# Attention and two gated MLPs on one core: v of the first batch loaded in contiguous pieces, transfer rates in the planner's prices, weight sums on VectorE, own tiles for the last results

## Chip, cores and metric

One NeuronCore of a Trainium2 chip runs the whole program in one launch. The metric is the device time of one execution in microseconds; lower is better. Engines are TensorE (PE), VectorE (DVE), ScalarE (ACT), GpSimd (POOL) and SyncE (SP, which issues most transfers).

## The reference

Three stages in float32 over 8 batches of 576 tokens. First linear attention with 8 heads of 64:

```python
q_s = softmax(q, axis=head_dim)
k_s = softmax(k, axis=seq)
kv = einsum('bhsd,bhse->bhde', k_s, v)
x = einsum('bhsd,bhde->bhse', q_s, kv)      # heads joined: x is [8, 576, 512]
```

Then an MLP with a gate that mixes the tokens:

```python
h = gelu(x @ w_in)                          # [576, 1024], halves u and v
v_n = (v - mean) / sqrt(var + 1e-6) * g_ln
v_s = einsum('ts,bsd->btd', w_sg, v_n) + b_sg
x = x + (u * v_s) @ w_out
```

Then one with a convolution of 3 taps along the tokens as its gate:

```python
h = relu(x @ w_in2)                         # [576, 1024]
out = (h * sigmoid(conv3(h, conv_w))) @ w_out2
```

## The kernel before

Every product keeps float32 accuracy by splitting each operand into a high and a low part and adding three products (`mm3`, line 472). So weights and activations must be split before PE can use them: ACT rounds the high part, another engine subtracts it to get the low part (names end in h and l).

Phase 1, up to about 562 us, runs attention and the first MLP batch by batch. Phase 2 runs the second MLP. There, batches 0 and 1 multiply by w_in2 directly (`h2`, line 1229). Batches 2 to 7 use a scheme of seven instead of eight block products (`quad`, line 1420); it needs sums of blocks of the weights, which `weight_sums(c)` (line 1327, for c = 0 and 1) forms once while batches 0 and 1 are still being computed: 4 sums high + low (`tk<-w2h,w2l`), 4 differences (`tk<-tk,tk`), then 3 splits into tn0, tn1, tn2, of which ACT makes the high and POOL the low part. That makes 11 operations on POOL for each c.

No engine's order is written by hand. The program calls engines through recorders; a planner (class `Plan`, lines 149 to 424) keeps every operation as a node with its dependences, prices it (`price`, line 216), derives due times backwards from the end (`deadlines`), and simulates all engines and the transfer lanes to choose at each moment what each engine takes next (`order`, line 280). `emit` (line 417) then issues the real instructions in that order. So nearly all instructions show the line of `emit`, L424, and are told apart by tile names here; and a change of one price can move instructions on every engine. A load on SP is priced at 1.9 us + KB / 200 (line 225), and the lanes are taken as busy for KB / 200 (line 339).

At the start, k of batch 0 is loaded in four tiles (sgl), q in five (sgh), v in one (vt, `load_v(0)`, line 897), then the weights (vnh, vnl, xh, xl, wsl are buffers that weights are staged in). The tile vt has 65 columns for each head, the last one holds ones, so that v fills 64 of 65 columns: its load writes into strided places. DVE takes maxima and sums for the softmaxes (sm), POOL subtracts and multiplies on q (sgh), PE transposes q (acc<-one,sgh; `s_qt`, line 949). Then `back_kv` (line 702) multiplies k and v (mm<-vt,kt), `xt` (line 743) multiplies by q, and `w_job` (line 1009) splits the weights of the first MLP in pieces, with PE, ACT, DVE and POOL taking part (on PE: mm<-vnh,one with mm<-wAh,neg). The first product of that MLP is mm<-wAh,xh.

At the end, `evac` (line 1261) copies each finished block of the result from PSUM to a tile ot, of which there are two, by turns on ACT and DVE, and SP stores it. The last block comes out in five such pieces.

Of the kernel before, what the change touches and what calls it, by code (L numbers as in the profile page):

```python
# [11 lines left out]
F32 = mybir.dt.float32  # L12
# [13 lines left out]
CFG = {'dord': 'qqkqqkqwkkwwv', 'start': 'kaaatabbktbkbqkTawtqbqtQvwwvxxqxswxlwLc', 'gh': 'aaa', 'x2': 'nnn', 'hvl': [6, 5, 3], 'qs': 'ppppd', 'qm': 'pppdp', 'vb': 2, 'gb': 2, 'kt': 'dddd', 'sgl': 'dppp', 'rh': 'pd', 'sw': 'ada', 'sl': 'ada', 'gl': 'ddd'}  # L26
FAR = 90.0
FIRST = 2
SUMS = ((0, 6), (1, 2))
YB = 4  # L30
GUARD = 1.125 * 2.0 ** -15
# [103 lines left out]


class Node:
    __slots__ = ("eng", "name", "args", "kw", "cost", "lat", "deps", "succ", "late", "unit", "shared", "table", "kb", "i", "left", "ready", "done", "t", "hook", "due")


class Engine:
# [7 lines left out]
class Plan:  # L149
# [66 lines left out]
    def price(self, n, out, ins):  # L216
        size = lambda v: int(np.prod(v.shape[1:]))
        views = ins + ([out] if isinstance(out, View) else [])
        cols = max(size(v) for v in views)
        psum = any(v.tile.space == "psum" for v in views)  # L220
        e, name = n.eng, n.name
        if e == "sp":
            v = views[0]
            n.kb = v.ids.size * 4 / 1024
            n.cost, n.lat = 0.42, 1.9 + n.kb / 200
        elif e == "pe":
            m = size(out)
            if name == "transpose":
                n.cost = 0.22
            elif ins[0].tile.dtype == F32:  # L230
                n.cost = 0.09 if m == 65 else 0.71 if m == 512 else 0.19
            else:
                n.cost = max(0.111, 0.0045 + m * 0.000447)
            n.lat = n.cost + 0.17
        elif e == "act":
            n.cost = (0.155 if psum else 0.195) + cols * 0.00085
            if isinstance(n.kw.get("scale"), View) or isinstance(n.kw.get("bias"), View):
                n.cost += 0.05 + min(cols, 500) * 0.0001
            n.lat = n.cost + 0.07
            f = args_func(n)  # L240
            n.table = {"Gelu_apprx_tanh": "g", "Exp": "e", "Sigmoid": "s"}.get(f)
        elif e == "pool":
            if "dma" in name:
                n.cost, n.lat = 1.2, 20.0
                return
            if "tensor" in name:
                wide = any(o[0] == "to_broadcast" for v in views for o in v.ops)
                n.cost = 0.95 if cols == 1 else 0.2 + cols * (0.0008 if name == "tensor_copy" else 0.00164 if wide else 0.0021)
            else:
                n.cost = 0.05 + cols * 0.0009  # L250
            n.lat = n.cost + 0.1
            n.shared = True
        else:
            two = sum(v.tile.space != "psum" for v in ins) > 1 and not psum and name in ("tensor_tensor", "scalar_tensor_tensor")
            fast = not psum and name in ("tensor_scalar", "tensor_copy") and out.tile.dtype == F32
            n.cost = 0.15 + cols * (0.0062 if name == "reciprocal" else 0.00055 if fast else 0.00104)
            if len(ins) > 2 or (fast and len(ins) > 1):
                n.cost += min(cols, 500) * 0.00013
            n.lat = n.cost + 0.07
            n.shared = (two or fast) and cols > 60  # L260
# [19 lines left out]
    def order(self):  # L280
# [41 lines left out]
        def start(n, t):  # L322
            cost, lat = n.cost, n.lat
            if n.eng == "act" and n.table and n.table != table[0]:
                cost, lat, table[0] = cost + 1.28, lat + 1.28, n.table
            if n.eng == "dve" and n.shared and poolend[0] > t:
                more = min(cost, poolend[0] - t) * 1.0
                cost, lat = cost + more, lat + more
            if n.eng == "pool":
                if vecend[0] > t:  # L330
                    more = min(0.5, vecend[0] - t)
                    cost, lat = cost + more, lat + more
                poolend[0] = t + cost
            if n.eng == "dve" and n.shared:
                vecend[0] = t + cost
            if n.eng == "sp":
                heapq.heappush(events, max(t, wire[0] - 1.0) + 0.01)
                s = max(t + 0.4, wire[0])
                wire[0] = s + n.kb / 200
                lat = wire[0] + 1.9 - t  # L340
                heapq.heappush(events, wire[0] - 0.99)
            n.t, n.done = t, t + lat
            free[n.eng] = t + cost
            out.append(n)
            heapq.heappush(events, free[n.eng])
            heapq.heappush(events, n.done)
            release(n, "start", t)
            release(n, "end", n.done)
# [84 lines left out]
def attn_gated_conv_kernel(ctx, tc, q, k, v, q0, k0, w_in, g_ln, w_sgT, b_sg, w_out, w_in2, conv_w, w_out2, out):  # L433
# [144 lines left out]
    def load_q(b):  # L578
        for c in range(4):
            sp.dma_start(q_tile(b, c), q[b, :, c * 512:c * 512 + 512])  # L580
# [4 lines left out]
    def load_v(b):  # L585
        sp.dma_start(vt[:, :, :, 0:64], v[b])
# [307 lines left out]
        sp.dma_start(k0t[:, hps[i]], k0[:, hps[i]])  # L894
    for i in range(5):
        sp.dma_start(q0t[:, qts[i]], q0[:, qts[i]])
    load_v(0)

    for e in range(2):
        pool.memset(r32(rhs2[e]), 0.0)  # L900
# [96 lines left out]
    for hp in range(4):  # L997
        s_qt(hp)
    s_qtl()
    load_q(1)  # L1000
    load_left(1)
    s_xl()
# [4 lines left out]
    xt_left(0)  # L1007
    xt_copy(0)
    def w_job(i):
        split(slots[ORDER[i]], *jobs[i], None)  # L1010

    ORDER = (4, 5, 0, 1, 2, 3, 0, 1, 2, 3, 0, 1)
    for i in range(4):
# [5 lines left out]

    def sg_split(c):  # L1020
        act.activation(sg["hi"][:, c], sgs[:, c % 2], AF.Copy)
        for hf in range(2):
            cs = slice(hf * HALF, hf * HALF + HALF)
            plan.begin()
            ps = mm_tile()[:, 0:HALF]
            part(ps, sgs[:, c % 2, cs], sg["hi"][:, c, cs])
            act.activation(sg["lo"][:, c, cs], ps, AF.Copy)
        if c < 3:
            sg_load(c + 2)
# [216 lines left out]
    def gate(b, fc, h, cv):  # L1246
# [11 lines left out]
        dve.tensor_tensor(zl, cv[:, 512:S], r32(zh), ALU.subtract)  # L1258
        y_t[b, fc] = (yh, yl)

    def evac(ps, dst, i=0):
        ot = p2.tile([128, DM], F32, tag="ot", bufs=2)
        if i % 2:
            dve.tensor_copy(ot, ps)
        else:
            act.activation(ot, ps, AF.Copy)
        for rows, d in dst:
            sp.dma_start(d, ot[rows])
# [58 lines left out]
    def weight_sums(c):  # L1327
        after = plan.last
        w11, w12, w21, w22, w3 = (tmp() for _ in range(5))
        for t, n in zip((w11, w12, w21, w22), ("11", "12", "21", "22")):  # L1330
            pool.tensor_tensor(t, r32(wq[n][0][:, c]), r32(wq[n][1][:, c]), ALU.add).deps[after.i] = "start"
        pool.tensor_tensor(w11, w12, w11, ALU.subtract)
        pool.tensor_tensor(w3, w22, w12, ALU.subtract)
        pool.tensor_tensor(w22, w22, w11, ALU.subtract)
        pool.tensor_tensor(w21, w21, w22, ALU.subtract)
        for t, (hi, lo) in zip((w11, w22, w21), tn):
            act.activation(hi[:, c], t, AF.Copy)
            pool.tensor_tensor(lo[:, c], t, r32(hi[:, c]), ALU.subtract)
        last.append(w3)

    def last_sum():
# [144 lines left out]
    while len(oq) > 1:  # L1486
        do_o()
    o2_pair(B - 1, range(NFC - 1))
    do_o()
    o2_pair(B - 1, [NFC - 1])  # L1490
    plan.emit()
# [52 lines left out]
```

## Time and profile before

| what | value |
|---|---|
| median of 3 runs | 963.08 us (961.0 to 966.03) |
| the profiled execution | 961.07 us |
| its span in the profile | 959.2 us (1.87 us lie outside) |
| PE busy | 926.0 us (97%), 6026 matmuls |
| DVE busy | 775.2 us (81%), 1455 instructions |
| ACT busy | 540.8 us (56%), 1113 instructions |
| POOL busy | 347.6 us (36%), 351 instructions |
| granted TensorE clock | 0.998 |
| transfers | 99.16 MB, lanes 35% busy |

Each execution ends when the slowest engine has ended and the last store has landed. Because PE is busy for 97% of the span, the time is PE's work plus PE's idle time; a stage in which another engine is nearly full shows where PE may have to wait. A row of a timeline tells the start in us, the duration, engine, line, operation, output<-input by tile names, and in brackets the idle time of that engine just before it and who ended it.

### The profile page before, as it was taken

How to read it: one execution, taken by the hardware profiler on the slowest of the kernel's cores; microseconds unless marked ns; L12 is line 12 of the kernel's file. 1: busy time of each engine (PE TensorE's matmuls, PEld its weight loads, DVE VectorE, ACT ScalarE, POOL GpSimd, SP SyncE). 2: the span in 40 equal slices, each digit the busy share in tenths (PEclk: the TensorE clock that was granted, in tenths of full speed). 3: DMA queues.
4: the chain of work that ended last, by engine and by line, in shares of the span. 5: the costliest groups of instructions: out<-in, count | busy, mean ns of one | idle time of the engine just before them, and what ended most of it. 6: DMA issues, size and time to landing. Idle time of an engine off the chain costs nothing.

```text
span 959.2 us, 16062 instructions
## 1 busy us (share of the span) xinstructions
PE 926.0 (97%) x6026; PEld 818.8 (85%) x6026; DVE 775.2 (81%) x1455; ACT 540.8 (56%) x1113; POOL 347.6 (36%) x351
## 2 busy tenths in 40 slices
PE   5999989999999999999999999999999999999996
PEld 4568877989988889888899998888989889988985
DVE  6987899889879889898766359998788968896773
ACT  6775553745646456737533225445666756766662
POOL 5425354555626636646543030851211202020000
PEclk9999999999999999999999999999999999999999
DMA  9551524182473553813457671002111211021001
GB/s 280 163 185 56 163 71 112 51 208 52 154 178 102 162 138 114 212 39 118 92 162 207 198 213 51 35 12 71 35 50 44 73 33 68 26 72 34 23 23 55
DMA packets 54246, 99.16 MB, mean 103 GB/s; under 512 B 5268, under 2 KB 28820, under 8 KB 52376
## 3 DMA queue, kind: packets, MB, share of 16 engines
q1 hardware_dynamic: 50472, 89.88, 30.0%
q0 software_dynamic: 3696, 8.26, 4.8%
q8 instruction: 47, 0.77, 0.3%
q14 instruction: 31, 0.25, 0.1%
HBM read 62.59 MB, written 35.53 MB: 102 GB/s over the span
## 4 chain that ended last, share of the span: by engine, by line
PE 74%; DVE 15%; ACT 4%; DMA 3%; issue 2%; SPq 0%; POOL 0%; ACTq 0%; DVEq 0%
PE mm L424 50%; PE acc L424 24%; DVE cv L424 4%; DMA wsl<-in_w_in 2%; DVE wsl L424 2%; DVE xl L424 1%; DVE scr L424 1%; DVE yl L424 1%; ACT L424 1%; DVE gl L424 1%; DVE vnl L424 1%; DVE sm L424 1%; DMA sgh<-in_q 0%; ACT vnh L424 0%; DVE lx L424 0%
## 5 line engine op out<-in xcount | busy, mean ns | idle before, releaser
L424 DVE SCALAR_TENSOR_TENSOR cv<-h,cw,cv 128x576 f32<-128x576 f32 x128 | 120.0, 937 | 22.1 <-ACT cv L424 20.5
L424 PE MATMUL acc<-wAh,yl 128*128 128x512 f32 x256 | 101.9, 398 | 1.2 <-DVE yl L424 1.2
L424 PE MATMUL acc<-wAh,yh 128*128 128x512 f32 x256 | 101.1, 395 | 1.5 <-ACT yh L424 1.2
L424 PE MATMUL acc<-wAl,yh 128*128 128x512 f32 x256 | 101.1, 395 | 0.0
L424 PE MATMUL mm<-xh,w2h 128*128 128x288 f32 x280 | 82.9, 296 | 0.0
L424 PE MATMUL mm<-xl,w2h 128*128 128x288 f32 x280 | 82.4, 294 | 0.0
L424 PE MATMUL mm<-xh,w2l 128*128 128x288 f32 x280 | 82.4, 294 | 0.0
L424 PE MATMUL mm<-sgh,vnh 128*128 128x288 f32 x256 | 81.2, 317 | 1.1 <-DVE u L424 0.8
L424 PE MATMUL mm<-xh,wAh 128*128 128x288 f32 x256 | 79.7, 311 | 2.0 <-DVE xl L424 1.2
L424 PE MATMUL acc<-gh,wouth 128*128 128x288 f32 x256 | 80.9, 316 | 0.0
L424 ACT ACTIVATE cv<-cv 128x576 f32<-128x576 f32 x64 | 43.7, 683 | 62.7 <-DVE cv L424 62.6
L424 PE MATMUL acc<-gl,wouth 128*128 128x288 f32 x256 | 76.3, 298 | 0.7 <-DVE gl L424 0.6
L424 PE MATMUL mm<-sgh,vnl 128*128 128x288 f32 x256 | 75.7, 296 | 0.8 <-DVE vnl L424 0.8
L424 PE MATMUL acc<-gh,woutl 128*128 128x288 f32 x256 | 75.8, 296 | 0.0
L424 PE MATMUL mm<-xh,wAl 128*128 128x288 f32 x256 | 75.5, 295 | 0.0
L424 PE MATMUL mm<-xl,wAh 128*128 128x288 f32 x256 | 75.5, 295 | 0.0
L424 PE MATMUL mm<-sgl,vnh 128*128 128x288 f32 x256 | 75.4, 294 | 0.0
L424 POOL TENSOR_TENSOR q<-q,qm 128x512 f32<-128x512 f32 x56 | 61.6, 1125 | 26.1 <-DVE qm L424 22.2
L424 POOL TENSOR_TENSOR wsl<-wsl 128x256 f32<-128x256 f32 (+1 forms) x66 | 48.4, 733 | 57.9 <-DVE wsl L424 31.9
L424 POOL TENSOR_TENSOR kt<-kt,scr 128x512 f32<-128x512 f32 (+1 forms) x42 | 48.5, 1181 | 49.5 <-PE mm L424 24.0
L424 ACT ACTIVATE gh<-u 128x288 fp32r<-128x288 f32 x64 | 28.2, 441 | 67.3 <-DVE u L424 67.1
L424 POOL TENSOR_TENSOR xf<-xf 128x576 f32<-128x576 f32 x12 | 21.8, 1821 | 118.9 <-DVE xl L424 90.2
(276 smaller groups left out, 2960.3 us busy)
## 6 DMA issues: line engine op xcount, KB each, us to landing
vt<-in_v SPq DMA_DIRECT2D x8, 1152.0 KB, 8.9
x2d<-x2s SPq DMA_DIRECT2D x16, 576.0 KB, 3.8
out<-ot SPq DMA_DIRECT2D x32, 256.0 KB, 2.1
kt<-in_k SPq DMA_DIRECT2D x7, 1152.0 KB, 5.3
x2d<-xl POOLq DMA_DIRECT2D x7, 1152.0 KB, 11.2
xf<-x2d SPq DMA_DIRECT2D x7, 1152.0 KB, 5.9
q<-in_q SPq DMA_DIRECT2D x28, 256.0 KB, 3.0
wsl<-in_w_in SPq DMA_DIRECT2D x16, 256.0 KB, 3.7
```

The source lines that it names most:

```text
L424: getattr(self.real[n.eng], n.name)(*[val(a) for a in n.args], **{k: val(v) for k, v in n.kw.items()})
```

## The change

The planner gives each transfer a rate of its own: 125 KB per us for the strided load of v into vt, 250 for all others, in place of 200 for all. The v of batch 0 is loaded in five contiguous pieces into buffers that later hold q (tags q0 to q4), and `v_stage` copies them into vt with five copies on POOL. The sums of the weights are made on DVE (`WS`) instead of POOL. For the last result's five pieces, `evac` takes own tiles, which are slices of the operand buffers xf and xg, instead of ot. `JOBS` and `SGL` hold only 'n' and leave `w_job` and `sg_split` as they were (their hunks are left out here).

```diff
@@ -26,6 +26,10 @@
...
 FAR = 90.0
 FIRST = 2
+WS = 'd'
+JOBS = 'nnnnnnnnnnnn'
+SGL = 'nnnn'
+VST = 'pppp'
 SUMS = ((0, 6), (1, 2))
 YB = 4
 GUARD = 1.125 * 2.0 ** -15
@@ -222,7 +226,8 @@
         if e == "sp":
             v = views[0]
             n.kb = v.ids.size * 4 / 1024
-            n.cost, n.lat = 0.42, 1.9 + n.kb / 200
+            n.rate = 125 if any(o[0] == '__getitem__' and len(o[1]) > 3 for o in v.ops if isinstance(o[1], tuple)) and v.tile.key.startswith('vt') else 250
+            n.cost, n.lat = 0.42, 1.9 + n.kb / n.rate
         elif e == "pe":
             m = size(out)
             if name == "transpose":
@@ -336,7 +341,7 @@
             if n.eng == "sp":
                 heapq.heappush(events, max(t, wire[0] - 1.0) + 0.01)
                 s = max(t + 0.4, wire[0])
-                wire[0] = s + n.kb / 200
+                wire[0] = s + n.kb / n.rate
                 lat = wire[0] + 1.9 - t
                 heapq.heappush(events, wire[0] - 0.99)
             n.t, n.done = t, t + lat
@@ -894,7 +899,20 @@
         sp.dma_start(k0t[:, hps[i]], k0[:, hps[i]])
     for i in range(5):
         sp.dma_start(q0t[:, qts[i]], q0[:, qts[i]])
-    load_v(0)
+    vst = [(4 * c, at.tile([128, 512 if c < 4 else 256], F32, tag=f"q{c}", bufs=2)) for c in range(5)]
+    for c, (g, t) in enumerate(vst):
+        n = min(4, 18 - g)
+        sp.dma_start(t, v[0, :, g:g + n].rearrange("p g e d -> p (g e d)"))
+
+    def v_stage():
+        for c, (g, t) in enumerate(vst):
+            n = min(4, 18 - g)
+            dst_, src_ = vt[:, g:g + n, :, 0:64], t.rearrange("p (g e d) -> p g e d", g=n, e=2)
+            if VST[min(c, 3)] == 'a':
+                act.activation(dst_, src_, AF.Copy)
+            else:
+                E[VST[min(c, 3)]].tensor_copy(dst_, src_)
+
     for e in range(2):
         pool.memset(r32(rhs2[e]), 0.0)
@@ -997,6 +1015,7 @@
     for hp in range(4):
         s_qt(hp)
     s_qtl()
+    v_stage()
     load_q(1)
     load_left(1)
     s_xl()
@@ -1258,8 +1279,13 @@
         dve.tensor_tensor(zl, cv[:, 512:S], r32(zh), ALU.subtract)
         y_t[b, fc] = (yh, yl)
+    out_t = []
+
     def evac(ps, dst, i=0):
-        ot = p2.tile([128, DM], F32, tag="ot", bufs=2)
+        if out_t:
+            ot = out_t.pop()
+        else:
+            ot = p2.tile([128, DM], F32, tag="ot", bufs=2)
         if i % 2:
             dve.tensor_copy(ot, ps)
         else:
@@ -1328,14 +1354,14 @@
         after = plan.last
         w11, w12, w21, w22, w3 = (tmp() for _ in range(5))
         for t, n in zip((w11, w12, w21, w22), ("11", "12", "21", "22")):
-            pool.tensor_tensor(t, r32(wq[n][0][:, c]), r32(wq[n][1][:, c]), ALU.add).deps[after.i] = "start"
-        pool.tensor_tensor(w11, w12, w11, ALU.subtract)
-        pool.tensor_tensor(w3, w22, w12, ALU.subtract)
-        pool.tensor_tensor(w22, w22, w11, ALU.subtract)
-        pool.tensor_tensor(w21, w21, w22, ALU.subtract)
+            E[WS].tensor_tensor(t, r32(wq[n][0][:, c]), r32(wq[n][1][:, c]), ALU.add).deps[after.i] = "start"
+        E[WS].tensor_tensor(w11, w12, w11, ALU.subtract)
+        E[WS].tensor_tensor(w3, w22, w12, ALU.subtract)
+        E[WS].tensor_tensor(w22, w22, w11, ALU.subtract)
+        E[WS].tensor_tensor(w21, w21, w22, ALU.subtract)
         for t, (hi, lo) in zip((w11, w22, w21), tn):
             act.activation(hi[:, c], t, AF.Copy)
-            pool.tensor_tensor(lo[:, c], t, r32(hi[:, c]), ALU.subtract)
+            E[WS].tensor_tensor(lo[:, c], t, r32(hi[:, c]), ALU.subtract)
         last.append(w3)
     def last_sum():
@@ -1486,6 +1512,8 @@
     while len(oq) > 1:
         do_o()
     o2_pair(B - 1, range(NFC - 1))
+    out_t.extend(p2.tile([128, KC, S], F32, tag="xf")[:, i, 0:512] for i in range(4))
+    out_t.append(p2.tile([128, S], F32, tag="xg")[:, 0:512])
     do_o()
     o2_pair(B - 1, [NFC - 1])
     plan.emit()
```

On SP, at the start of the program (sgl is k, sgh is q, vt and the tiles q are v, vnh and the rest are weights). Before:

```order
L424 DMA sgl_89<-in_k 128x576 x2
L424 DMA sgh_98<-in_q 128x512
L424 DMA vt_85<-in_v 128x36x64
L424 DMA sgh_98<-in_q 128x256
L424 DMA vnh_121<-in_w_in 128x1024
L424 DMA vnl_124<-in_w_in 128x1024
```

Now:

```order
L429 DMA sgl_89<-in_k 128x576 x2
L429 DMA sgh_98<-in_q 128x512
L429 DMA sgh_98<-in_q 128x256
L429 DMA q_0_119<-in_v 128x512
L429 DMA q_0_122<-in_v 128x512
L429 DMA q_0_126<-in_v 128x512
L429 DMA q_0_128<-in_v 128x512
L429 DMA q_0_130<-in_v 128x256
L429 DMA vnh_133<-in_w_in 128x1024
L429 DMA vnl_136<-in_w_in 128x1024
```

The fifth tile of q (128x256) stands ahead of v, and five issues of v stand where one stood, still ahead of the weights.

On DVE, at the start (sm<-sgh are maxima and sums of q; of the two in one row before, the first is the sum of the third tile, the second the maximum of the fourth, and in the new order these two have changed places). Before:

```order
L424 TENSOR_SCALAR sm_117<-sm_117 128x8
L424 TENSOR_REDUCE sm_117<-sgl_89 128x1
L424 TENSOR_REDUCE sm_117<-sgh_98 128x8
L424 TENSOR_REDUCE sm_117<-sgl_89 128x1
L424 TENSOR_REDUCE sm_117<-sgh_98 128x8 x2
L424 RECIPROCAL sm_117<-sm_117 128x8
```

Now:

```order
L429 TENSOR_REDUCE sm_117<-sgl_89 128x1
L429 TENSOR_REDUCE sm_117<-sgh_98 128x8
L429 TENSOR_REDUCE sm_117<-sgl_89 128x1
L429 TENSOR_REDUCE sm_117<-sgh_98 128x8 x2
L429 TENSOR_SCALAR sm_117<-sm_117 128x8
L429 RECIPROCAL sm_117<-sm_117 128x8
```

The small TENSOR_SCALAR has moved behind the maximum of q's fourth tile.

On DVE, in batch 1 of phase 2 (cv is the convolution, yh and yl the gated result, tk and tn the sums of the weights). Now:

```order
L429 TENSOR_TENSOR cv_5694<-cv_5694,h_0_4981 128x576
L429 TENSOR_TENSOR tk_5992<-w2h_4967,w2l_5005 128x512
L429 TENSOR_TENSOR tk_6000<-w2h_4967,w2l_5005 128x512
L429 TENSOR_TENSOR yl_5840<-cv_5694,yh_5823 128x512
L429 TENSOR_SCALAR cv_5742<-h_0_5662,cw_861 128x576
L429 SCALAR_TENSOR_TENSOR cv_5742<-h_0_5662,cw_861,cv_5742 128x576 x2
L429 TENSOR_TENSOR yLl_5777<-cv_5694,yLh_5752 128x64
L429 TENSOR_TENSOR tk_5992<-tk_6000,tk_5992 128x512
L429 TENSOR_TENSOR tk_6056<-w2h_4967,w2l_5005 128x512
```

These are the first sums: they stand in ones and twos between the steps of the convolution, from there on to the first block products of batch 2; before, no sum stood on DVE.

## Rows read from the trace of the kernel before

**Rows 1.** Windows: stretch; length, busy us (instructions) of each engine; clock, DMA share, GB/s
```profile
0.00:959.20 959.20, 926.04 (x6026) 818.84 (x6026) 775.21 (x1455) 540.80 (x1113) 347.61 (x351) 1.00 0.35 103
0.00:40.00 40.00, 27.50 (x156) 16.34 (x157) 31.24 (x61) 28.37 (x54) 18.02 (x30) 1.00 0.73 232
600.00:640.00 40.00, 38.74 (x227) 34.12 (x226) 39.55 (x35) 17.25 (x38) 31.84 (x20) 1.00 0.07 27
640.00:660.00 20.00, 20.00 (x117) 17.82 (x116) 19.31 (x29) 11.14 (x24) 3.75 (x2) 1.00 0.00 1
```

**Rows 2.** Timeline of ACT at the end: start, us, operation, [idle before <-releaser]
```profile
951.99 0.60 ACT L424 ACTIVATE ot<-acc 128x512 f32<-128x512 f32 x1 [2.15 <-DMA out<-ot]
954.73 0.60 ACT L424 ACTIVATE ot<-mm 128x512 f32<-128x512 f32 x1 [2.14 <-DMA out<-ot]
```

**Rows 3.** What PE waits for, 40 to 560 us: total us, times, longest
```profile
PE mm L424 <- DVE u L424: 2.8, 2, 2.0
```

**Rows 4.** Timeline of PE at the end
```profile
951.61 0.39 PE L424 MATMUL mm<-wAh,yLl 128*128 128x512 f32 x1
```

**Rows 5.** Groups on tile tk: min/median/max ns, first and last start
```profile
L424 POOL TENSOR_TENSOR tk<-w2h,w2l x8: 1300/1804/1816, 567.4 to 635.3; 128x512 f32<-128x512 f32 x8
```

**Rows 6.** Timeline of DVE, 566 to 576 us
```profile
566.22 4.89 DVE L424 SCALAR_TENSOR_TENSOR cv<-h,cw,cv 128x576 f32<-128x576 f32 x2
...
574.39 0.82 DVE L424 SCALAR_TENSOR_TENSOR cv<-h,cw,cv 128x576 f32<-128x576 f32 x1
575.12 0.68 DVE L424 TENSOR_TENSOR yl<-cv,yh 128x512 fp32r<-128x512 f32 x1
```

**Rows 7.** What PE waits for, 560 to 660 us
```profile
PE acc L424 <- DVE yl L424: 1.2, 2, 0.7
```

**Rows 8.** Timeline of PE near 576 us
```profile
575.86 0.50 PE L424 MATMUL acc<-wAh,yl 128*128 128x512 f32 x1 [0.70 <-DVE yl L424]
```

**Rows 9.** Timeline of SP at the start
```profile
4.50 0.68 SPq L424 DMA_DIRECT2D vt<-in_v  x1
5.23 7.49 SPq L424 DMA_DIRECT2D sgh<-in_q  x1
```

**Rows 10.** DMA issues of the first 22 us: count, KB, median us to landing
```profile
vt<-in_v SPq DMA_DIRECT2D x1, 1152.0 KB, 10.5
```

**Rows 11.** Windows at the start, columns as in rows 1
```profile
4.00:10.00 6.00, 2.09 (x8) 1.43 (x8) 5.05 (x9) 4.78 (x9) 4.59 (x6) 1.00 1.02 331
10.00:13.00 3.00, 2.04 (x9) 1.64 (x10) 2.97 (x9) 2.41 (x5) 0.47 (x1) 1.00 1.04 218
```

**Rows 12.** Timeline of DVE at the start
```profile
11.19 1.26 DVE L424 TENSOR_REDUCE sm<-sgh 128x8 f32<-128x512 f32 x2
...
15.88 1.25 DVE L424 TENSOR_TENSOR sgh<-sgh,sm 128x512 f32<-128x512 f32 x1
```

**Rows 13.** Timeline of POOL at the start
```profile
1.32 0.53 POOL L424 MEMSET kvd<- 128x512 f32 x1
...
12.53 4.04 POOL L424 TENSOR_TENSOR sgh<-sgh,sm 128x512 f32<-128x512 f32 x4 [3.20 <-DVE sm L424]
```

**Rows 14.** What PE waits for, 0 to 40 us
```profile
PE acc L424 <- POOL sgh L424: 2.1, 3, 1.0
PE mm L424 <- POOL xh L424: 0.8, 2, 0.6
PE mm L424 <- DVE xl L424: 0.5, 1, 0.5
```

**Rows 15.** Timeline of PE at the start
```profile
20.10 1.83 PE L424 MATMUL mm<-vt,kt 128*64 128x65 f32 x40
...
28.35 1.08 PE L424 MATMUL mm<-vnh,one 128*128 128x512 f32 x2
...
30.41 1.02 PE L424 MATMUL mm<-vnl,one 128*128 128x512 f32 x2
...
38.69 0.82 PE L424 MATMUL mm<-wAh,xh 128*128 128x512 f32 x1
```

More of the change, by code (lines that the diff above doesn't have):

```diff
@@ L137 @@
 class Node:
-    __slots__ = ("eng", "name", "args", "kw", "cost", "lat", "deps", "succ", "late", "unit", "shared", "table", "kb", "i", "left", "ready", "done", "t", "hook", "due")
+    __slots__ = ("eng", "name", "args", "kw", "cost", "lat", "deps", "succ", "late", "unit", "shared", "table", "kb", "i", "left", "ready", "done", "t", "hook", "due", "rate")
 class Engine:
@@ L1009, in w_job @@
     def w_job(i):
-        split(slots[ORDER[i]], *jobs[i], None)
+        split(slots[ORDER[i]], *jobs[i], None if JOBS[i] == 'n' else (E[JOBS[i]], E[JOBS[i]]))
     ORDER = (4, 5, 0, 1, 2, 3, 0, 1, 2, 3, 0, 1)
@@ L1021, in sg_split @@
         act.activation(sg["hi"][:, c], sgs[:, c % 2], AF.Copy)
-        for hf in range(2):
+        if SGL[c] != 'n':
+            E[SGL[c]].tensor_tensor(sg["lo"][:, c], sgs[:, c % 2], r32(sg["hi"][:, c]), ALU.subtract)
+        for hf in range(2 if SGL[c] == 'n' else 0):
             cs = slice(hf * HALF, hf * HALF + HALF)
```

## The prediction, on record before the changed kernel ran

> **What bounds the kernel now.** I read the busy times by stage first, then what TensorE (PE) waits for in each stage, then the single rows around those waits. PE is busy for 926.0 of 959.2 us, at a granted clock of 1.00 in every stage shown [rows 1]: that is the upper of its two levels, 2.4 GHz, so the clock has nothing to give. The change removes no matmul, so only PE's 33.2 us of idle time can be won. The first 40 us hold 12.5 of them, the stretch from 600 to 640 in phase 2 holds 1.3 [rows 1]. Behind the last matmul, two evictions each stand more than 2 us behind a store [rows 2]. The rest is scattered between 40 and 560 us; the largest single wait there is 2.0 us [rows 3].
>
> **The tail.** Before, the last five results share two buffers. ScalarE (ACT) stands 2.15 us until a store has emptied its buffer, evicts at 951.99, stands 2.14 us more and begins the last eviction at 954.73 [rows 2]. With five own tiles it waits for PE alone. PE's last matmul begins at 951.61 and takes 0.39 [rows 4], so that eviction can begin at about 952.0: **-2.7 us**. The stores behind it have the same size as before. Bounds: -2.2, if one more store still in flight delays the last by half a microsecond (a quarter of the 2.15 that a store holds ACT up here), to -2.8.
>
> **The weight sums.** 22 operations (11 for each c) leave GpSimd (POOL), where eight of one kind take 1.80 us as a median [rows 5], and go to VectorE (DVE), where a two-input 128x512 operation takes 0.68 [rows 6]. That is 22 x 0.68 = 15.0 us more work for an engine that is busy for 39.55 of the 40 us from 600 to 640 [rows 1]. What speaks for it: beside POOL's sums DVE's own instructions are long. Two conv steps took 4.89 us there, one without POOL 0.82 [rows 6]. From 600 to 640 DVE ran 35 instructions in 39.55 us, 1.13 each; from 640 to 660, with POOL nearly idle, 29 in 19.31, 0.67 each [rows 1]. At 0.67 the 35 would take 23.3, so about 16 us there are stretch, and 4.89 - 2 x 0.82 = 3.2 more at 566: about 19. Four of POOL's operations in these stretches (on xf and xg) stay; at 1.1 us of stretch each I leave 4 for them. So 15 us are freed and 15.0 spent: DVE's load stays level, its instructions become short, and a step in the chain of sums takes 0.7 instead of 1.8 us. Of the 1.2 us that PE waits on yl in this part of the program [rows 7], 0.70 is one wait at 575.86 [rows 8], behind the stretched part at 566 to 574, and the new order puts no sum there: it goes. Of the 1.3 us that PE idles from 600 to 640 [rows 1] I take about half, 0.7: **-1.4 us**. Bounds: -2.0, all of it, to +0.7, one more 0.68 sum ahead of a yl for which PE waits.
>
> **The start.** Three things move.
> (a) Transfers. The strided load of v, issued at 4.50, takes 10.5 us to land, so v is there at 15.0, and the issue behind it, of q's fifth tile, holds SyncE (SP) for 7.49 us [rows 9, 10]. Only then do the first weights go out. From 4 to 10 us the lanes carry 331 GB/s, from 10 to 13 us, when v is nearly alone, 218, just as full [rows 11]. In the new order q's fifth tile goes first, then v in five contiguous pieces, then the weights. In the 5 us from 10 to 15 the old load moves some 1.1 MB at 218; at 331 that takes 3.3 us, so v would be there at 13.3 or, with q's tile no longer behind it, somewhat before. I take 13; the weights follow at once instead of after 12.7.
> (b) VectorE's list. At 11.19 it does the sum of q's third tile and then the maximum of the fourth, for which POOL waits until 12.53 [rows 12, 13]. In the new order that maximum stands ahead, and a TENSOR_SCALAR behind: POOL's four multiplications, 12.53 to 16.57, move to about 11.5 to 15.5. PE waits for exactly these, three waits of 2.1 us in all [rows 14]. Its transposes of q end at 20.10 before [rows 15], at about 19.1 after.
> (c) The copies. POOL lays v into place with five COPYs behind the multiplications. No such row exists before. Below: a MEMSET of 128x512 takes 0.53; above: a two-input operation of that size 4.04 / 4 = 1.01 [rows 13]. 4.5 times that size gives 2.4 to 4.6 us. A copy reads one input, so I take the upper middle, 0.85, or 3.8 us in all: 15.5 to 19.3. The first attention product then begins at about 19.4 instead of 20.10.
> From there to 28.35 PE works without a wait. Four groups that split weights follow. One with nothing in its way takes 30.41 - 28.35 = 2.06 us [rows 15]; four would take 8.2, but took 10.3, to 38.69 [rows 15], with waits of 0.8 on POOL's xh and 0.5 on VectorE's xl [rows 14], because the weights came late and VectorE's jobs on them queued up behind the attention's sums. Now two of these jobs stand ahead of those sums. I take 27.7 + 8.9 = 36.6 for the first matmul of the MLP instead of 38.69: **-2.0 us**, 0.7 from the earlier attention and 1.3, the size of those waits, from the groups. Best: all three kinds of wait go, -3.4. Worst: POOL is not earlier and a copy costs as much as a sum, so v is ready at 16.57 + 4.6 = 21.2, and everything is +1.1 late.
>
> The Trainium skill (SBUF — State Buffer, section "Who interferes with whom") says that a VectorE instruction with two inputs in SBUF and a GpSimd instruction that reads SBUF shut each other out for the length of the one that began first. The 4.89 us above agree with it. The same rule speaks against (c), which gives GpSimd five new reads of SBUF; what that would do is part of the first rival, from rows.
>
> **The middle.** The new rates reorder every list, but on PE, DVE and ACT between 40 and 560 us mostly neighbours change places, and v of batch 1 now goes out right behind its k. I take 0; the bound either way is the largest wait there, 2.0 us [rows 3].
>
> **The sum.** The profiled execution took 961.07 us. 961.07 - 2.7 - 1.4 - 2.0 = 955.0. The median of the three runs, 963.08, is 2.0 above it: **957.0** as a median. All best bounds together give -10.2, all worst ones +1.6.
>
> **Rivals.**
> 1. The start gives nothing. POOL's copies lie beside VectorE's two-input instructions, and those wait: the multiplication of q's fourth tile beside POOL's took 1.25 us, an operation of that size without POOL 0.68 [rows 6, 12]. With such a hit or two, and copies at 1.01, the start is +1.1. For it: the copies are the last thing that the attention products wait for. Against: they read one input each, and the max moves ahead. Time: 961.07 - 2.7 - 1.4 + 1.1 = 958.1, as a median 960.1: no change. Chance 0.2.
> 2. Slower: VectorE becomes the bound from 600 to 655. The sums cost 15.0; it had 0.45 us to spare up to 640 and 0.7 up to 660 [rows 1]. If the stretch S that goes with POOL's sums is small, PE waits for 15.0 - 1.1 - S. That outweighs the 4.7 of tail and start once S is below 9.2; at S = 0 it is +13.9 - 4.7 = +9.2, as a median 972.3. Against: S by the rows is about 15, and a conv step takes 0.82 as soon as POOL rests. Chance 0.05.
> 3. The tail does not do what it says. The new tiles are slices of x's operand buffers; should ACT wait there for a store after all (four results lie in one buffer), the -2.7 goes: 957.7, as a median 959.7, no change. Against: the slices do not overlap. Chance 0.05.
>
> **How the numbers follow.** The forecast has 0.7. About 0.5% (4.8 us) is what a measurement of this kernel can tell from no change, so faster means below 958.3. The forecast lies 1.3 us under that: of its 0.7 I put 0.57 there, since tail and sums alone give -4.1 and any gain of 0.7 at the start is enough. Faster 0.57, same 0.13 + 0.2 + 0.05 = 0.38, slower 0.05. The range goes from 952.0, all the best bounds together (952.9) and 0.9 less, since the three runs before lie 5 us apart, to 962.0, which takes in rivals 1 and 3 with the middle's 2 us on top; rival 2 stays out.
>
> **What would show it.** Right: the last eviction follows PE at once, with no store before it; no POOL row on tk; conv steps of 0.82 between 600 and 640; the first weight issued before 10 us and the MLP's first product about 2 us earlier. Wrong: PE waiting for vt or POOL at 19 to 21 us; DVE at 20 of 20 and PE waits on yl of over 2 us in all between 600 and 655; new waits of a microsecond or more between 40 and 560 us.

## The result and the profile after

Six executions of the changed kernel have a median of 952.85 us (951.52 to 956.76), six of the kernel before, taken with them, 961.59 us (959.54 to 966.03). The ratio is 0.9909 with a 95% interval of 0.989 to 0.9928: 0.91% faster, 8.7 us. The forecast was 957.0 us, -6.1 on 963.08. A second series of the same kernel, below, gave 0.9925 (0.9904 to 0.9946). Here and below a ratio is not exactly the quotient of the two medians; the two differ most in run 7 (0.9916 and 0.9933) and run 6 (0.9977 and 0.9992).

The profiled execution took 954.37 us with a span of 952.6, 6.6 less than before. Its windows, with the columns of [rows 1] (length, busy us of PE, weight loads, DVE, ACT, POOL, then clock, DMA share, GB/s):

```profile
0.00:952.60 952.60, 926.21 (x6026) 821.09 (x6026) 772.91 (x1477) 543.69 (x1113) 317.80 (x334) 1.00 0.35 104
0.00:40.00 40.00, 28.31 (x155) 17.07 (x156) 31.82 (x61) 27.93 (x54) 21.92 (x36) 1.00 0.81 261
600.00:640.00 40.00, 40.00 (x240) 36.17 (x239) 38.75 (x63) 18.70 (x40) 3.45 (x2) 1.00 0.07 27
```

PE does the same 6026 matmuls; its idle time went from 33.2 to 26.4 us. From 600 to 640 DVE runs 63 instructions in 38.75 us, where it ran 35 in 39.55 [rows 1], and PE no longer waits there.

To see where the 6.6 us come from I follow PE through points that every version passes: the first matmul of the first MLP (mm<-wAh,xh), the first of phase 2 (mm<-xh,w2h), the first block product on tn0, the last matmul, ACT's last eviction and the end of the span. All are start times, read from the timelines and the groups; phase 2 and tn0, for instance, begin at 561.84 and 654.80 before, at 560.76 and 650.68 after.

| stretch | before, us | after, us | difference | forecast |
|---|---|---|---|---|
| start to first MLP matmul | 38.69 | 39.00 | +0.31 | -2.0 |
| from there to phase 2 | 523.15 | 521.76 | -1.39 | 0 |
| from there to the first product on tn0 | 92.96 | 89.92 | -3.04 | -1.4 |
| from there to PE's last matmul | 296.81 | 296.81 | 0.00 | 0 |
| last matmul to last eviction | 3.12 | 0.42 | -2.70 | -2.7 |
| last eviction to the end of the span | 4.42 | 4.69 | +0.27 | 0 |

The differences add up to the 6.6 us. The last row goes with the pieces of v and not with the tiles: it is 4.7 in all eight profiled executions with pieces and 4.4 in all six with one load. So the tail is what was forecast, the sums gave twice as much, the middle gave something, and the start gave nothing in this execution.

**Tail.** ACT's timeline, against [rows 2]:

```profile
946.52 0.60 ACT L429 ACTIVATE xf<-acc 128x512 f32<-128x512 f32 x1 [0.80 <-PE acc L429]
947.91 0.60 ACT L429 ACTIVATE xf<-mm 128x512 f32<-128x512 f32 x1 [0.80 <-PE mm L429]
```

Both evictions wait for PE alone; PE's last matmul began at 947.49.

**Sums.** Two groups on tile tk (min/median/max ns; first and last start), and DVE's timeline, which answers to [rows 5, 6]:

```profile
L429 DVE TENSOR_TENSOR tk<-w2h,w2l x8: 683/685/1930, 596.1 to 651.4; 128x512 f32<-128x512 f32 x8
L429 DVE TENSOR_TENSOR tk<-tk,tk x8: 684/684/691, 602.6 to 653.4; 128x512 f32<-128x512 f32 x8
```

```profile
596.67 1.93 DVE L429 TENSOR_TENSOR tk<-w2h,w2l 128x512 f32<-128x512 f32 x1
598.52 1.92 DVE L429 TENSOR_TENSOR yl<-cv,yh 128x512 fp32r<-128x512 f32 x1
600.37 0.51 DVE L429 TENSOR_SCALAR cv<-h,cw 128x576 f32<-128x576 f32 x1
600.91 1.67 DVE L429 SCALAR_TENSOR_TENSOR cv<-h,cw,cv 128x576 f32<-128x576 f32 x2
602.50 0.22 DVE L429 TENSOR_TENSOR yLl<-cv,yLh 128x64 fp32r<-128x64 f32 x1
602.64 0.68 DVE L429 TENSOR_TENSOR tk<-tk,tk 128x512 f32<-128x512 f32 x1
```

A sum takes 0.68 us as forecast, and two conv steps 1.67 instead of 4.89. Each of the two rows of 1.9 lies beside one of POOL's operations on x that stayed (at 596.14 and 598.13).

**Start.** SP, POOL and PE, against [rows 9, 13, 15]:

```profile
5.07 4.00 SPq L429 DMA_DIRECT2D q<-in_v  x5
9.49 0.33 SPq L429 DMA_DIRECT2D vnh<-in_w_in  x1
```

```profile
11.91 1.04 POOL L429 TENSOR_TENSOR sgh<-sgh,sm 128x512 f32<-128x512 f32 x1 [1.71 <-DVE sm L429]
13.36 3.06 POOL L429 TENSOR_TENSOR sgh<-sgh,sm 128x512 f32<-128x512 f32 x3 [0.41 <-DVE sm L429]
16.38 3.47 POOL L429 COPY vt<-q 128x512 f32<-128x512 f32 x5
```

```profile
20.00 2.77 PE L429 MATMUL mm<-vt,kt 128*64 128x65 f32 x40
...
29.20 1.08 PE L429 MATMUL mm<-vnh,one 128*128 128x512 f32 x2
...
31.25 1.02 PE L429 MATMUL mm<-vnl,one 128*128 128x512 f32 x2
...
39.00 0.82 PE L429 MATMUL mm<-wAh,xh 128*128 128x512 f32 x1
```

The first weight goes out at 9.49 instead of behind 12.7, and the five copies take 3.47 us (forecast 3.8). Yet the attention begins at 20.00 against 20.10, and its first 40 matmuls take 2.77 us instead of 1.83. The second forty, at 23.06, took 1.83 again. The groups on tile vt show why (min/median/max ns), for the first 22.2 us and behind them:

```profile
L429 PE MATMUL mm<-vt,kt x34: 258/315/370, 20.0 to 22.2; 128*64 128x65 f32 x30, 64*64 64x65 f32 x4
```

```profile
L429 PE MATMUL mm<-vt,kt x50: 218/222/312, 22.1 to 24.7; 128*64 128x65 f32 x38, 64*64 64x65 f32 x12
```

The kernel before:

```profile
L424 PE MATMUL mm<-vt,kt x40: 218/222/272, 20.1 to 21.7; 128*64 128x65 f32 x32, 64*64 64x65 f32 x8
```

The same matmul takes 315 ns up to about 22.2 us and 222 behind it; before, all 40 from 20.1 to 21.7 took 222 as a median. So the clock rose to its upper level of 2.4 GHz about 2 us later in this execution, and 0.94 us went with it. The clock column of the windows shows 1.00 there and does not tell this.

**Middle.** PE before, three of its waits:

```profile
63.05 0.40 PE L424 MATMUL mm<-sgh,neg 128*128 128x288 f32 x1 [1.20 <-ACT sgh L424]
98.46 3.58 PE L424 MATMUL mm<-vt,kt 128*64 128x65 f32 x80 [1.25 <-ACT kt L424]
127.23 0.50 PE L424 MATMUL mm<-wAh,xh 128*128 128x512 f32 x1 [2.03 <-DVE u L424]
```

Of the two waits before 100 us neither is left; from the first MLP matmul to phase 2 PE idles for 9.3 us in place of 10.8. But there is something that no row of before shows. PE's timeline and the windows of the changed kernel, in which the third number from the end is the clock:

```profile
124.38 0.58 PE L429 MATMUL mm<-wAh,xh 128*128 128x512 f32 x1 [2.06 <-DVE u L429]
124.75 0.63 PE L429 MATMUL mm<-wAl,xh 128*128 128x512 f32 x1
```

```profile
122.00:124.00 2.00, 0.32 (x3) 0.08 (x1) 1.97 (x4) 0.00 (x0) 2.00 (x3) 1.00 0.00 0
124.00:126.00 2.00, 1.62 (x4) 1.29 (x5) 2.00 (x4) 0.83 (x2) 1.69 (x3) 0.66 0.00 0
126.00:128.00 2.00, 2.00 (x6) 1.58 (x5) 1.94 (x4) 0.00 (x0) 0.00 (x0) 0.50 0.00 0
128.00:130.00 2.00, 2.00 (x13) 1.81 (x13) 0.35 (x1) 0.96 (x2) 0.00 (x0) 0.98 0.00 0
```

PE waited 2.06 us for DVE, and when it went on, the granted clock was 0.50, the lower level of 1.2 GHz, for about 3.4 us; below I call this the fall of the clock. The kernel before has nearly the same wait, 2.03 us at 127.23, and no fall in its profiled execution.

### The profile page after: what moved, and what is told of

It reads as the page before. It is cut to its first block, busy times and chain, and to the rows that moved or that the text cites. A ratio compares the mean times of both kernels' runs of the same rounds, so it can differ in the third digit from the quotient of the medians.

```text
span 952.6 us, 16062 instructions
## 1 busy us (share of the span) xinstructions
PE 926.2 (97%) x6026; PEld 821.1 (86%) x6026; DVE 772.9 (81%) x1477; ACT 543.7 (57%) x1113; POOL 317.8 (33%) x334
## 4 chain that ended last, share of the span: by engine, by line
PE 85%; DVE 9%; DMA 2%; ACT 2%; issue 1%; POOL 0%; SPq 0%; ACTq 0%
PE mm L429 57%; PE acc L429 28%; DVE wsl L429 2%; DVE sm L429 1%; DMA wsl<-in_w_in 1%; DVE scr L429 1%; DMA wsl<-in_w_out 1%; DVE r L429 1%; DVE vnl L429 1%; DVE xl L429 1%; DVE gl L429 1%; DMA sgh<-in_q 1%; DVE lm L429 0%; DVE u L429 0%; DVE x2s L429 0%
## 5 line engine op out<-in xcount | busy, mean ns | idle before, releaser
L429 DVE SCALAR_TENSOR_TENSOR cv<-h,cw,cv 128x576 f32<-128x576 f32 x128 | 111.9, 875 | 17.3 <-ACT cv L429 15.5
L429 POOL TENSOR_TENSOR wsl<-wsl 128x256 f32<-128x256 f32 (+1 forms) x66 | 50.7, 768 | 60.5 <-DVE wsl L429 23.7
L429 DVE TENSOR_TENSOR cv<-cv,h 128x576 f32<-128x576 f32 x64 | 52.2, 816 | 13.0 <-ACT cv L429 12.2
```

The costliest lines, as they stand in the source:

```text
L429: getattr(self.real[n.eng], n.name)(*[val(a) for a in n.args], **{k: val(v) for k, v in n.kw.items()})
```

## The experiments

The main theory after the result: the sums and the tail are worth 3.04 and 2.70 by themselves; v in pieces is worth nothing, because something else sets the start; the middle comes from the order that the rates set. The rival for the sums: the gain came with the order, not with the engine.

**1. Own tiles alone.** The kernel before, with only the two hunks of the diff on `out_t`; the second is shown above, the first is

```diff
     def evac(ps, dst, i=0):
-        ot = p2.tile([128, DM], F32, tag="ot", bufs=2)
+        if out_t:
+            ot = out_t.pop()
+        else:
+            ot = p2.tile([128, DM], F32, tag="ot", bufs=2)
```

> Only the own tiles for the last five results, all else as before. Theory (the two waits of 2.15 us on stores were the whole loss): the last eviction on ACT begins 0.4 us after PE's last matmul begins instead of 3.1; PE ends where it ended before, near 951.6; the span falls by 2.5 to 2.7, the time by 0.28%. Rival (the stores themselves are the end: with the waits gone six of them queue up): the last eviction is early, but the span falls by less than 1.5 us.

Median 959.10 against 962.85 us, ratio 0.9963 (0.9947 to 0.998). ACT's last evictions:

```profile
953.02 0.60 ACT L424 ACTIVATE xf<-acc 128x512 f32<-128x512 f32 x1 [0.80 <-PE acc L424]
954.42 0.60 ACT L424 ACTIVATE xf<-mm 128x512 f32<-128x512 f32 x1 [0.80 <-PE mm L424]
```

PE's last matmul began at 953.99: 0.43 us from there to the last eviction, and 4.4 on to the end of the span, as before. The stores don't queue up; the rival falls. This profiled execution as a whole is only 0.3 us shorter than that of before, because PE ended 2.4 us later: its clock rose at 23 us (before, at 20), and it fell to 0.50 for 3.4 us at 128.9, behind the same wait, with the same instructions in the same order up to the tail. That was not expected and is taken up below.

**2. Sums on VectorE alone.** The kernel before, with `pool.` replaced by `dve.` in `weight_sums`.

> Only the 22 weight sums on VectorE, all else as before. Theory (POOL's sums stretched VectorE's instructions, and each stall of PE costs its idle time and about 0.27 us more): from the first matmul of phase 2 to the first block product on tn0 it takes about 90 us instead of 93.0, no PE wait on yl, time -3 us or -0.3%. Rival A (VectorE becomes the bound): 93 or more, with PE waits on yl of over 2 us. Rival B (the gain in that stretch came with the order that the new rates set, not with the engine): 93 as before.

Median 958.49 us, ratio 0.9955 (0.994 to 0.997). The two points in the groups of PE (first and last start):

```profile
L424 PE MATMUL mm<-xh,w2h x280: 292/296/300, 562.1 to 929.8; 128*128 128x288 f32 x140
```

```profile
L424 PE MATMUL mm<-xh,tn0h x32: 293/296/298, 652.0 to 874.8; 128*128 128x288 f32 x32
```

89.9 us, with no wait of PE of 0.2 us or more between 560 and 660. Rivals A and B both fall: the engine alone gives the 3.05 us.

**3. The changed kernel with the sums back on POOL.**

```diff
-WS = 'd'
+WS = 'p'
```

> The changed kernel with the 22 weight sums back on POOL. Theory: the same stretch takes 93 us again instead of 89.9, conv steps beside POOL's sums are near 1.8 us again, the time is 3 us above the changed kernel, that is about 0.6% below before. Rival B (order, not engine): the stretch stays at 90 and the time at that of the changed kernel.

Median 955.71 us, ratio 0.9921 (0.9899 to 0.9942). The stretch takes 93.4 us (559.8 to 653.2), 3.5 more than in the changed kernel. What PE waits for there, and two conv steps on DVE:

```profile
PE acc L429 <- DVE ot L429: 1.2, 1, 1.2
PE acc L429 <- DVE yl L429: 0.8, 2, 0.5
PE acc L429 <- ACT yh L429: 0.5, 1, 0.5
```

```profile
600.22 3.61 DVE L429 SCALAR_TENSOR_TENSOR cv<-h,cw,cv 128x576 f32<-128x576 f32 x2
```

So in this stretch the engine decides with both orders, and the order does not. The whole time does not show it: the ratio 0.9921 lies between the changed kernel's 0.9909 and 0.9925, where 3 us above it was expected. At an equal clock it does: the executions with a mean granted clock of 0.999 take 954.76 to 955.80 us here and 950.91 to 952.04 in the changed kernel's two series.

**4. The changed kernel with v strided in one piece.** `vst` and `v_stage` are taken out, `load_v(0)` is back; sums, tiles and rates stay.

> The changed kernel with v of batch 0 loaded in one strided piece again, and no copies. Theory (the start hangs on VectorE's chain of maxima and sums on q, not on v): the transposes of q still end near 20 and the first matmul of the first MLP comes near 39, within 0.6 of both kernels, so the pieces are worth nothing there; time within 1 us of the changed kernel. Rival (the pieces were needed, since in the new order v is what the attention waits for): PE waits on vt and the first MLP matmul comes at 40 or later, time 1 to 2 us above the changed kernel.

Median 951.21 us, ratio 0.988 (0.9859 to 0.9901): lower than the changed kernel, and outside "within 1 us". PE at the start:

```profile
14.96 3.02 PE L429 MATMUL mm<-vt,kt 128*64 128x65 f32 x40 [1.71 <-DMA vt<-in_v]
17.91 3.36 PE L429 MATMUL acc<-one,sgh 128*128 128x128 f32 x16
```

The first MLP matmul came at 37.37. Both sides were wrong: with the strided load priced at its measured rate, the planner puts the first product of k and v in front of the transposes of q, into a time in which PE had to wait for q anyway. With the pieces it does so in none of the eight profiled executions. Why is not shown; run 10 below has v in place early and still keeps the product behind the transposes.

**5. Rates alone.** The kernel before with the two rates in `price` and `order`.

> Only the two transfer rates in the planner's prices; v of batch 0 strided, sums on POOL, two buffers at the end. Theory (the new rates by themselves put the first product of k and v ahead of the transposes of q on PE, into a wait, as in the run with v strided): the first MLP matmul comes at 37.4 instead of 38.7, phase 2 begins 3 to 4 us earlier than before, the sums' stretch takes 93 us and the last eviction begins 3.1 us behind PE's last matmul; time -3 to -4 us (-0.4%). Rival (the rates only shuffle lists): phase 2 begins within 1 us of before, no change in time.

Median 958.86 us, ratio 0.9961 (0.9943 to 0.9979). First MLP matmul at 37.16, again with the product in front of the transposes; phase 2 begins at 557.52, 4.3 us earlier than before; stretch of the sums 93.3; 3.6 us to the last eviction. The theory holds; the 4.3 and the 3.6 are each half a microsecond or less above what it said. Of the 4.3, 2.8 lie between the first MLP matmul and phase 2, and not in PE's idle time, which is 10.75 us there as before (10.80): PE's busy time for the same matmuls fell from 512.35 to 509.61 us. PE waits there 12 times instead of 21; at 0.27 us for each wait on top of its idle time (worked out below) that makes an estimated 2.4 of the 2.7 us.

**6. Pieces alone.** Of the changed kernel only `vst` and `v_stage`; price 200, sums on POOL, two buffers.

> Only v of batch 0 in five pieces with copies on POOL; old price of 200, sums on POOL, two buffers at the end. Theory (the pieces land early but are copied behind POOL's work on q, so v is in place at about 20, later than the strided load had it, and the attention products begin behind the transposes as before): first MLP matmul at 38.4 to 39.4, phase 2 begins within 1 us of before, no change in time. Rival (the pieces are where the early weights come from): first MLP matmul at 37.5 or earlier, time -1 us or more.

Median 961.09 against 961.90 us, ratio 0.9977 (0.9957 to 0.9996), over nine executions; a tenth, of 2792 us, is left out. First MLP matmul at 40.74, later than in any other version (clock up at 23 us, and the weight groups took 10.85 us, see below); but phase 2 began at 561.69, as before, so some 2 us came back in the middle, in spite of a fall of the clock there. That the start gains nothing holds; that nothing else moves does not.

**7. Old price with all the rest.** `n.rate = 200` in the changed kernel.

> The changed kernel with the old price of 200 KB per us for all transfers: the pieces, the sums on VectorE and the own tiles stay. Theory (the parts add up): 3.05 from the sums, 2.7 from the tail, nothing from the pieces, so 5.8 us below before (-0.6%), phase 2 beginning within 1 us of before. Rival (the new order by the rates carries a part of the gain of the sums): the sums' stretch takes 91 us or more.

Median 955.44 us, ratio 0.9916 (0.9887 to 0.9944). Stretch of the sums 89.9: the rival falls. Phase 2 began at 559.19, 2.6 us earlier than before, not within 1: the pieces by themselves reorder the middle, too. By the ratio the time is 8.1 us below before where 5.8 was expected, but the interval takes 5.8 in. With the pieces in place, the rates add little that can be measured: 0.9916 without, 0.9909 with them.

**8. Copies on ACT** instead of POOL.

```diff
-VST = 'pppp'
+VST = 'aaaa'
```

> The changed kernel with the five copies of v on ACT, which stood idle for 2.96 us behind 14.6, instead of POOL. Theory A (VectorE's chain on q ends at 17 and the transposes at 20 whatever v does, and in this list the product stands behind them): first MLP matmul within 0.6 of 39.0, time as the changed kernel. Theory B (POOL's copies beside VectorE's instructions hold the start): VectorE's multiplication at 15.7 takes 0.7 instead of 1.2 and the first MLP matmul comes at 38.2 or earlier.

Median 950.79 us (950.63 to 950.90), ratio 0.9872 (0.9842 to 0.9903). First MLP matmul at 36.42, with the clock up at 20.2 instead of 22.2; the clock is worth some 0.9 of the 2.6 us to the changed kernel, so A falls; but DVE's multiplication of q's fourth tile still took 1.25 us, beside POOL's multiplications, so B's reason falls, too.

**9 to 11. The changed kernel, the copies on ACT (8) and the strided version (4) again**, on one chip, because the profiled executions differed in their transfers and clock.

> The changed kernel itself once more, beside the two variants that came out lower, on one chip. Expected by the ledger of stages: first MLP matmul between 38 and 39, depending on when the clock rises (22.2 before: a rise near 20 would give 38.1); 89.9 us for the sums' stretch; 0.4 us from PE's last matmul to the last eviction; a ratio of 0.990 to 0.992. If the difference to the two variants was chance, all three ratios agree within 0.2%.

> The changed kernel with the five copies of v on ACT, again. Theory (POOL takes its list in order, so the copies stand behind its multiplications on q until 16.4 and v is in place at 19.9; on ACT they ran from 11.3 to 15.4): first MLP matmul 1 us or more ahead of the changed kernel at an equal rise of the clock, time 0.2% to 0.35% below the changed kernel. Rival (the earlier run had earlier transfers by chance): first MLP matmul at 38 or later and the same time as the changed kernel.

> The changed kernel with v strided, again. Theory (the strided load had v in place at 15.0, so the first product ran in front of the transposes, in time that PE had to wait anyway): first MLP matmul near 37.4, time 0.15% to 0.3% below the changed kernel. Rival (chance): the same time as the changed kernel.

Ratios: the changed kernel 0.9925 (0.9904 to 0.9946; median 953.95 us, 950.91 to 957.04), copies on ACT 0.9898 (0.9881 to 0.9914; 951.41), strided 0.9904 (0.9888 to 0.9921; 951.98). The first lies just outside the 0.990 to 0.992 that was expected. PE in the changed kernel, then with the copies on ACT:

```profile
19.46 2.92 PE L429 MATMUL mm<-vt,kt 128*64 128x65 f32 x40
...
28.81 1.08 PE L429 MATMUL mm<-vnh,one 128*128 128x512 f32 x2
...
38.61 0.81 PE L429 MATMUL mm<-wAh,xh 128*128 128x512 f32 x1
```

```profile
20.05 4.38 PE L429 MATMUL mm<-vt,kt 128*64 128x65 f32 x80
28.73 1.08 PE L429 MATMUL mm<-vnh,one 128*128 128x512 f32 x2
...
37.45 0.81 PE L429 MATMUL mm<-wAh,xh 128*128 128x512 f32 x1
```

The clock rose at the same time, near 22 us, in both. The attention ends at 28.8 in both, although ACT had v in place at 15.95 (its last three copies: 14.51 and 1.44 us): so the copies on POOL do not hold the attention, against what I expected of this run. Nearly all of the difference of 1.16 us lies in the four weight groups behind it: 9.80 against 8.72. These durations repeat to 0.02 us in every profiled execution of one list (the order that the planner gives each engine), and they follow the list: 10.33 before (also in runs 1 and 2), 10.85 and 10.86 with the old price and the pieces (runs 6 and 7), 9.80 to 9.82 with the new rates (changed kernel, runs 3, 4, 5), 8.72 with the copies on ACT. They do not follow the loading: in runs 4 and 5 the first weight goes out at 12.62 and 12.37, in the changed kernel at 9.49, and the groups take the same; in run 7 it goes out at 8.68, and they take about 1.1 more. Which instruction of ACT's or DVE's list makes the last step I did not isolate. In the strided version the first MLP matmul came at 38.04 this time (37.4 expected), with the clock up at 22.4 instead of 20.8.

A part of the strided version's lead is the clock. Taken over both series, its six executions at a mean clock of 0.999 or more took 950.39 to 951.28 us, the changed kernel's five 950.91 to 952.04: medians 0.6 us apart, where the medians of all executions lie 1.6 to 2.0 apart.

**12. Copies on VectorE.** `VST = 'dddd'`.

> The changed kernel with the five copies of v on VectorE. Theory (VectorE's chain of maxima, sums and multiplications on q sets the end of the transposes): five copies of about 0.4 us in that chain push the transposes and the first MLP matmul back by 0.5 to 2 us against the run with the copies on ACT, to 37.5 or later, time at or above the changed kernel. Rival (only POOL's queue was the trouble, any other engine does): first MLP matmul within 0.4 us of the run with the copies on ACT.

Median 953.34 us, ratio 0.9923 (0.9903 to 0.9943). First MLP matmul at 38.46, 1.0 behind the copies on ACT: the theory's number holds. The first product begins at 20.57 instead of 20.05, as the theory has it, and the attention ends 0.39 later (29.12 instead of 28.73); the other 0.62 are the weight groups, 9.34 instead of 8.72. The median is that of the changed kernel, but all four executions had a mean clock of 0.999 or more (953.28 to 954.76 us), and at that clock the changed kernel took 952.04 at most.

So the version with the copies on ACT is the lowest found: its ratio is 0.37 and 0.27 points below that of the changed kernel in the two series, with intervals that overlap by about 0.001 each time. In both, its slowest execution (950.90 and 951.63) is below the changed kernel's median. From the strided version (0.9880 and 0.9904) it can't be told apart.

## Why the prediction was right, and where it was not

**Direction and size.** The ratio's 8.7 us and the forecast 6.1 agree in sign; 952.85 lies at the low end of 952.0 to 962.0. About 1.5 of the 4.1 us between 957.0 and 952.85 come from the base: the median before was 963.08 over three runs and 961.59 over six. The rest is errors that partly cancelled: the start gave nothing of its -2.0, while the sums gave 1.6 more and the middle, put at 0, gave 1.4. So the tail and the direction of the sums were foreseen, and that the total came out near was in part luck.

**The tail: right.** -2.70, forecast -2.7, and run 1 shows it alone. Rival 3 did not happen: four results in slices of one buffer wait for no store.

**The sums: the mechanism right, the size half.** The prediction took only half of PE's waits from 600 to 640 (0.7), and all of them went; and it took a wait to cost its idle time. It costs more. The timeline of PE after, around a wait that both kernels have, shows it:

```profile
934.83 0.39 PE L429 MATMUL acc<-wAl,yh 128*128 128x512 f32 x1
935.06 0.40 PE L429 MATMUL acc<-wAh,yl 128*128 128x512 f32 x1
936.15 0.50 PE L429 MATMUL acc<-wAh,yh 128*128 128x512 f32 x1 [0.70 <-ACT yh L429]
936.50 0.39 PE L429 MATMUL acc<-wAl,yh 128*128 128x512 f32 x1
```

Undisturbed, a matmul begins 0.23 us behind the one before it, although it lasts 0.39. From 935.06 to 936.50 two such steps took 1.44 us, where two undisturbed ones take 0.47: 0.97 us for a wait shown as 0.70. That is 0.27 more. The kernel before had four waits in the stretch, the one of 0.70 in [rows 8] and

```profile
624.17 0.50 PE L424 MATMUL acc<-wAh,yh 128*128 128x512 f32 x1 [0.25 <-DVE ot L424]
627.25 0.50 PE L424 MATMUL acc<-wAh,yh 128*128 128x512 f32 x1 [0.52 <-ACT yh L424]
628.48 0.50 PE L424 MATMUL acc<-wAh,yl 128*128 128x512 f32 x1 [0.49 <-DVE yl L424]
```

In all that is 1.96 us; with 4 x 0.27 it makes 3.04, and run 2 and the changed kernel show -3.05 and -3.04. Run 3 bears it out: its four waits of 0.26, 1.18, 0.50 and 0.49 us give 3.51 in this way, and its stretch is 3.49 longer than the changed kernel's. Rival 2 (VectorE as the bound) did not happen: DVE was still busy for 38.75 of 40 us from 600 to 640, but PE did not wait there. The rule of the Trainium skill that the prediction cites (SBUF — State Buffer, "Who interferes with whom") fits run 3 against the changed kernel: two conv steps take 3.61 us beside POOL's sums and 1.67 without.

**The start: the step that failed.** The forecast was -0.7 for the attention and -1.3 for the groups.
- The max in front did move the instruction that waits for it from 12.53 to 11.91. But of the "four multiplications" of the prediction only this one, a subtraction, waits for the max; the three real multiplications wait for DVE's sums and reciprocals, in front of which the TENSOR_SCALAR now stood, and began at 13.36 instead of 13.53. The chain on DVE ended nearly where it had: the multiplication of q's fourth tile began at 15.73 against 15.88 [rows 12]. PE's waits on POOL fell from 2.1 to 1.9 only. Over three profiled executions of each list the first product began at 20.1 to 20.3 with the list of before (before, runs 1 and 2) and at 19.5 to 20.0 with the changed one (changed kernel twice, run 3): some -0.5.
- The groups took 9.80 instead of 10.34: -0.54 where I had -1.3 (the 8.9 of the prediction should have been 9.0). "because the weights came late" was wrong: the first weight went out 3.3 us earlier, and the groups became only half a microsecond shorter; runs 4 and 5 have the same 9.81 without the earlier weights. Another list (copies on ACT) takes another 1.1 us off; the list, not the loading of the weights, set it.
- The late rise of the clock took 0.94 back. The prediction had read the 1.00 of the clock column as "the clock has nothing to give"; no row of before showed that the rise can vary, and no term stood for it.

Rival 1 named the right outcome (the start gives nothing) for a reason that did not decide it. Beside a copy the multiplication of q's fifth tile did take 0.82 us instead of 0.42, but PE goes from the transposes into the first product at 20.00 without a wait, and with the copies on ACT the attention ended at the same time.

**The middle: 0 was wrong by more than the fall of the clock hides.** It was -1.39 with the fall of the clock in it. The strided version had the same list twice, without the fall 520.36 us for this stretch, with it 521.78: 1.4 us. Run 1 against before, the same list in this stretch, with it and without: 524.11 and 523.15, 1.0 us. These are net: in run 1 the wait near 98.5 us was 0.95 shorter than before, for one. PE's busy time in the stretch shows the fall more directly, 1.5 us more with it in the strided version (511.04 and 509.56) and 1.4 in run 1 (513.71 and 512.35). So I estimate that without it the new order would have given 2.4 to 2.9 us. Runs 5 (2.8, without a fall) and 7 (2.9, in spite of one) show that either part of the change, the rates or the pieces, brings such a gain, and that the two don't add. The 0.27 us for each wait, found for the sums, fits here: the changed kernel has 16 waits in the stretch instead of 21 and 1.5 us less idle time, by estimate 2.9 us together. The premise that "only PE's 33.2 us of idle time can be won" is the step that failed here: in run 5 the order alone took 2.7 us out of PE's busy time. That fewer waits are the cause is worked out from the counts, and no run varies them alone.

The changed kernel's executions spread from 951.5 to 956.8. Those at 951.5 to 951.9 have a mean granted clock of 0.999, those from 953.8 up 0.997 or 0.998, so the clock has a part in it. But the two events measured here, 1.4 to 1.5 us for the fall and 0.94 for the late rise, make 2.4 and not 5; the rest of the spread is open, and only one of these executions has a trace.

## What to carry to other kernels

Where an engine is nearly full, look first at which of its instructions are long only because of a neighbour: here 15 us of added work on VectorE cost nothing, since the work beside it on GpSimd had stretched VectorE by more (from 560 to 660 its busy time fell from 92.2 to 87.2 us). Price a wait of a pipelined engine by the start of the next instruction against its undisturbed step, not by the idle time in the row, and count the waits as well as adding them up. And where a planner writes the lists, a corrected price is a change of its own, with its own run: here rates, sums and tiles without the pieces came out lower than all four together in both series (0.9880 and 0.9909; 0.9904 and 0.9925; the intervals overlap, and at an equal clock 0.6 us is left).

## What was not expected of the hardware

- A PE wait cost 0.27 us more than its idle time (0.97 for 0.70; 3.04 for four waits of 1.96; 3.49 for four of 2.43 in run 3).
- The granted clock fell to 0.50 for 3.4 us during or just behind a PE wait of 2.0 to 2.6 us near 120 to 129 us in 9 of 14 profiled executions (among them both of the changed kernel and run 1). The other five had such a wait, too, and no fall (before, runs 2, 4, 5 and 12). Where the same list ran with it and without, it added 1.4 and 1.5 us to PE's busy time and 1.0 and 1.4 to the stretch.
- The same matmuls in another order took 509.61 instead of 512.35 us of PE's busy time between the first MLP matmul and phase 2, with 12 waits instead of 21 and the same idle time (run 5 and before, neither with a fall).
- At the start the clock rose between 20.0 and 23.1 us, at different times in executions of the same instructions (20.0 before, 23.1 in run 1); the first MLP matmul came at 38.69 and 40.01. The clock column says nothing of this; the duration of a known matmul does (315 against 222 ns).
